# Turning attention's output with VectorE and SBUF transfers instead of TensorE, padded k and v tails, and g_norm folded into the weights

## The chip, the cores and the metric

One Trainium2 chip; the kernel runs on one of its cores. Times are device microseconds (us) of that core. Each kernel was run several times, and each experiment beside runs of the kernel before on the same chip. All profiled runs were in the fast state, and a ratio uses fast runs alone (one run each of `warm2` and `one_step` was slow; their medians include it). A ratio is the mean time of one kernel's fast runs over that of the kernel before's fast runs of the same rounds, with a 95% interval, so it is not quite the ratio of the medians that are quoted beside it. Edits are shown shortened to the lines that matter, with comments of mine behind `#`.

## The reference, cut to what matters

Eight batches, eight heads, 576 rows (S), head size 64. The convolution weights, `w_val` and `w_out` arrive as float64.

```python
kv  = einsum('bhsd,bhse->bhde', k, v)            # linear attention
raw = einsum('bhsd,bhde->bhse', q, kv)
x   = raw / sqrt(mean(raw*raw, -1) + 1e-6) * g_norm    # per head
x   = x.transpose(0, 2, 1, 3).reshape(B, S, 512)
gate = sigmoid(causal convolution of x, 5 taps per channel)
val  = x @ w_val
out  = (gate * val) @ w_out
```

## The kernel before

Everything downstream of x needs it turned: channels on partitions, rows along the free axis (`xT`). The 576 rows of a batch are four chunks of 128 and a tail of 64. TensorE turns a chunk against an identity, ScalarE copies it out of PSUM and multiplies by `g_norm` on the way:

```python
def turn_x(b, c):                                   # TensorE
    px = ps("tp", [P, NK, P], f"xTps{b}_{c}")
    for col in range(heads(c) * D // P):
        nc.tensor.transpose(px[:, col, :], st["x", b, c][:, col * P:(col + 1) * P], ident[:])
def keep_x(b, c):                                   # ScalarE
    nc.scalar.activation(out=xTs[b % 3][:, :, first:first + m], in_=px..., func=AF.Copy, scale=gcol[:])
```

The kernel does not write its instructions in program order. Each piece of work is entered into a planner with an engine, an assumed duration, a wanted time, what it needs and which buffers it takes. The planner lays out all pieces and the kernel then issues them in that order; each engine runs its own list strictly in order. This is the part of it that matters here (`t` counts in the assumed clock):

```python
plan.add("POOL", 1.75 * part, t + 2.3, powers, b, c, ...)      # rt = ss ** -0.5
plan.add("DVE",  0.7 * part,  t + 4.2, normalise, b, c, ...)   # x = raw * rt
plan.add("PE",   0.55 * part, t + 5.5, turn_x, b, c, ...)
plan.add("ACT",  0.72 * part, t + 6.2, keep_x, b, c, ...)
# [cut] the gate of a channel block: one ScalarE copy, four VectorE taps, one ScalarE sigmoid
# [cut] val (TensorE, 3 PSUM banks), gv = val * gate (VectorE, frees the bank), out (TensorE)
first = begin - (28.0 if b == 1 else 34.0)          # attention wanted 34 us ahead of val
attention(b + 1, first, 3.0, first - 8.0, first - 7.0)
gates(b + 1, first + 20.5, 6.5)
```

So a chain runs raw, square, ss, rt, x, xT, gate, taps, gv; and the fourth `val` of a batch needs the bank that the first `gv` gives back.

## Time and profile before

| | |
|---|---|
| time, median of 3 runs | 371.3 us |
| span of the profiled run | 367.9 us (timed at 369.6 us, so one of the fastest) |
| TensorE busy | 346.4 us, 94% of it |
| granted TensorE clock | 0.983 |

The prediction below shows the lines that carry the diagnosis. From the view by stretches of time (window in us, its length, TensorE's busy time and matmul count, granted clock, DMA share, GB/s): from the first `out` to the end TensorE idles 272.40 - 267.72 = 4.7 us.

```profile
95.50:367.90 272.40, 267.72 (x1316) 1.00 0.38 104
```

The timeline: start, length, engine, line, operation; in brackets the idle time just before and what ended it.

```profile
41.93 2.21 PE L481 MATMUL val<-xT,wval 128*128 128x288 f32 x8 [1.13 <-DVE gv L490]
...
75.75 3.63 PE L481 MATMUL val<-xT,wval 128*128 128x288 f32 x8 [5.01 <-DVE gv L490]
```

Behind a wait of 1.13 us eight instructions take 2.21 us, behind one of 5.01 us they take 3.63. (In the chain, where a piece ends when the next begins, such a group is the 1.94 us of the prediction; lengths of the timeline are compared with 2.21.)

### The profile page before, as it was taken

How to read it: one execution, taken by the hardware profiler on the slowest of the kernel's cores; microseconds unless marked ns; L12 is line 12 of the kernel's file. 1: busy time of each engine (PE TensorE's matmuls, PEld its weight loads, DVE VectorE, ACT ScalarE, POOL GpSimd, SP SyncE). 2: the span in 40 equal slices, each digit the busy share in tenths (PEclk: the TensorE clock that was granted, in tenths of full speed). 3: DMA queues.
4: the chain of work that ended last, by engine and by line, in shares of the span. 5: the costliest groups of instructions: out<-in, count | busy, mean ns of one | idle time of the engine just before them, and what ended most of it. 6: DMA issues, size and time to landing. Idle time of an engine off the chain costs nothing.

```text
span 367.9 us, 5562 instructions
## 1 busy us (share of the span) xinstructions
PE 346.4 (94%) x2065; PEld 234.1 (64%) x2065; DVE 215.9 (59%) x363; ACT 142.6 (39%) x253; POOL 72.4 (20%) x78
## 2 busy tenths in 40 slices
PE   4889899679799999999999999999999999999994
PEld 3677777557455784578546884678546884674441
DVE  2077998989825996927239765937249545920000
ACT  3377657535335335311353235213253335201111
POOL 0045035101430351004400350005300350000000
PEclk9969999989999999999999999999999999999998
DMA  6999975912017941793128903692121001201322
GB/s 216 318 303 351 278 222 190 276 37 64 10 48 203 269 122 40 219 276 91 30 64 250 288 22 94 173 298 59 29 66 50 2 0 50 65 2 29 86 71 72
DMA packets 43194, 49.02 MB, mean 133 GB/s; under 512 B 14475, under 2 KB 34975, under 8 KB 43167
## 3 DMA queue, kind: packets, MB, share of 16 engines
q1 hardware_dynamic: 43006, 48.67, 47.4%
q8 instruction: 16, 0.26, 0.3%
q14 instruction: 12, 0.09, 0.1%
q10 hardware_dynamic: 160, 0.00, 0.0%
HBM read 39.21 MB, written 9.44 MB: 132 GB/s over the span
## 4 chain that ended last, share of the span: by engine, by line
PE 85%; DMA 5%; SPq 3%; DVE 3%; ACT 2%; issue 1%; ACTq 0%
PE val L481 34%; PE out L500 33%; PE raw L398 8%; PE kv L329 6%; DMA v<-in_v_dram 4%; PE xTps L444 4%; SPq L193 1%; DVE gate L469 1%; SPq L203 1%; PE qTps L359 1%; DVE gv L490 1%; DMA out_dram<-ot 0%; SPq L246 0%; ACT L476 0%; ACT gate L476 0%
## 5 line engine op out<-in xcount | busy, mean ns | idle before, releaser
L481 PE MATMUL val<-xT,wval 128*128 128x288 f32 x512 | 135.5, 413 | 6.7 <-DVE gv L490 6.1
L500 PE MATMUL out<-wout,gv 128*128 128x512 f32 x288 | 126.4, 592 | 0.0
L469 DVE SCALAR_TENSOR_TENSOR gate<-xT,cwT,gate 128x576 f32<-128x576 f32 x128 | 102.9, 816 | 30.8 <-ACT gate L463 28.0
L481 PEld LDWEIGHTS val<-xT,wval 128*128 128x128 f32 x512 | 94.7, 192 | 33.5 <-DVE gv L490 7.2
L426 POOL TENSOR_TENSOR rt<-ss,mhalf 128x8 f32<-128x8 f32 (+1 forms) x40 | 63.9, 1603 | 225.1 <-DVE ss L420 225.1
L500 PEld LDWEIGHTS out<-wout,gv 128*128 128x128 f32 x288 | 53.5, 190 | 60.9 <-issue 60.7
L508 ACT COPY ot<-out 128x512 f32<-128x512 f32 x36 | 21.0, 583 | 82.0 <-PE out L500 49.9
L490 DVE TENSOR_TENSOR gv<-val,gate 128x288 f32<-128x288 f32 x64 | 28.8, 454 | 32.8 <-PE val L481 32.2
L398 PE MATMUL raw<-kvbd,qT 128*128 128x128 f32 (+1 forms) x320 | 41.2, 290 | 0.9 <-ACT kvbd L339 0.9
L451 ACT ACTIVATE xT<-xTps,gcol 128x512 f32<-128x512 f32 (+1 forms) x40 | 25.8, 644 | 39.2 <-PE xTps L444 39.2
L398 PEld LDWEIGHTS raw<-kvbd,qT 128*128 128x128 f32 (+1 forms) x320 | 37.1, 190 | 6.1 <-issue 3.6
L412 ACT ACTIVATE sq<-raw 128x512 f32<-128x512 f32 (+1 forms) x40 | 22.2, 555 | 37.4 <-PE raw L398 37.1
L476 ACT ACTIVATE gate<-gate 128x576 f32<-128x576 f32 x32 | 21.8, 682 | 35.3 <-DVE gate L469 35.2
L433 DVE TENSOR_TENSOR x<-raw,rt 128x512 f32<-128x512 f32 (+1 forms) x40 | 25.2, 629 | 17.2 <-POOL rt L426 17.0
L420 DVE TENSOR_REDUCE ss<-sq 128x8 f32<-128x520 f32 (+1 forms) x40 | 25.4, 634 | 16.0 <-ACT sq L412 15.7
L444 PE MATMUL xTps<-ident,x 128*128 128x128 f32 x144 | 22.3, 274 | 2.2 <-DVE x L433 2.2
L444 PEld LDWEIGHTS xTps<-ident,x 128*128 128x128 f32 x144 | 17.7, 141 | 10.2 <-issue 6.3
L329 PE MATMUL kv<-v,k 128*64 128x64 f32 x512 | 22.1, 230 | 1.7 <-DMA v<-in_v_dram 1.7
L329 PEld LDWEIGHTS kv<-v,k 128*64 128x64 f32 x512 | 17.9, 139 | 8.5 <-issue 7.3
L463 ACT ACTIVATE gate<-xT,cwT 128x576 f32<-128x576 f32 x32 | 22.2, 764 | 0.3
L347 DVE STREAM_TRANSPOSE qT<-q 128x576 f32<-128x576 f32 x24 | 18.0, 764 | 1.7 <-DMA q<-in_q_dram 1.7
L359 PE MATMUL qTps<-ident,q 128*64 128x128 f32 (+1 forms) x160 | 11.5, 306 | 4.7 <-DMA q<-in_q_dram 4.4
(50 smaller groups left out, 98.0 us busy)
## 6 DMA issues: line engine op xcount, KB each, us to landing
q<-in_q_dram SPq DMA_DIRECT2D x96, 140.0 KB, 4.3
out_dram<-ot SPq DMA_DIRECT2D x144, 64.0 KB, 1.7
k<-in_k_dram SPq DMA_DIRECT2D x16, 512.0 KB, 4.4
v<-in_v_dram SPq DMA_DIRECT2D x16, 512.0 KB, 6.4
q<-in_q_dram SPq DMA_DIRECT2D x4, 512.0 KB, 5.8
w_wval<-in_moe_w_val_dram SPq DMA_DIRECT2D x4, 512.0 KB, 7.9
w_wout<-in_moe_w_out_dram SPq DMA_DIRECT2D x4, 512.0 KB, 6.5
kl<-in_k_dram SPq DMA_DIRECT2D x16, 64.0 KB, 5.3
```

The source lines that it names most:

```text
L329: nc.tensor.matmul(kvp[r * D:(r + 1) * D, hp, :], st["k", b, half][:, h, j, :] if j < NJ else kl[r * T:(r + 1) * T, hp, :], st["v", b, hal ...
L398: nc.tensor.matmul(raw[row * m:(row + 1) * m, col * P:(col + 1) * P], st["qT", b][:, hp, c * P:c * P + m], kv_bd[b % 2][:, hp, :], start=T ...
L412: nc.scalar.activation(out=sq[:, 0:n, 0:D], in_=st["raw", b, c][:, 0:n * D].rearrange("p (h e) -> p h e", h=n), func=AF.Square,)
L420: nc.vector.reduce_sum(out=ss[:, 0:n], in_=st["sq", b, c][:, 0:n], axis=AX.X)
L426: nc.gpsimd.tensor_tensor(out=rt[:, 0:n], in0=st["ss", b, c][:, 0:n], in1=mhalf[:, 0:n], op=ALU.pow)
L433: nc.vector.tensor_tensor(out=x[:, 0:n * D].rearrange("p (h e) -> p h e", h=n), in0=st["raw", b, c][:, 0:n * D].rearrange("p (h e) -> p h ...
L444: nc.tensor.transpose(px[:, col, :], st["x", b, c][:, col * P:(col + 1) * P], ident[:])
L451: nc.scalar.activation(out=xTs[b % 3][:, :, first:first + m], in_=px.rearrange("p (k t) -> p k t", k=NK), func=AF.Copy, scale=gcol[:],)
L469: nc.vector.scalar_tensor_tensor(out=gate[:], in0=xTs[b % 3][:, jt, tap * TB:tap * TB + S], scalar=cwT[:, tap, jt:jt + 1], in1=gate[:], op ...
L481: nc.tensor.matmul(val[:], wval[:, kc, jt * P:(jt + 1) * P], xTs[b % 3][:, kc, HALO + n * SV:HALO + (n + 1) * SV], start=(kc == 0), stop=( ...
L490: nc.vector.tensor_tensor(out=gv[:, jt, first:first + SV], in0=st["val", b, jt, n][:], in1=st["gate", b, jt][:, n * SV:(n + 1) * SV], op=A ...
L500: nc.tensor.matmul(po[:], gv[:, jt, c * P:(c + 1) * P], wout[:, jt, :], start=(jt == 0), stop=(jt == NK - 1),)
```

## The change

Its intent: TensorE is the bound, so take work from it.

- For batches 2 to 7 the four full chunks of x are no longer turned by TensorE. VectorE turns each 32x32 block in place (`y`), and 16 SBUF-to-SBUF transfers per batch, issued by GpSimd, put the blocks where `xT` wants them. For that the rows must lie in another order, so q's turn is cut from one instruction into five.
- The 64-row tails of k and v are padded with zeros to 128 partitions, so that their matmuls have the shape of the others.
- `g_norm` goes into the convolution weights and `w_val`, as the multiplication sat in ScalarE's copy, which goes.
- To make room, buffers of x go from 3 to 2, of gate from 5 to 4, of the float64 weights from 4 to 3.

```diff
-tails = [[const.tile([P, HP, D], FP32, ...
+tails = [[const.tile([P, H, D], FP32, ...          # rows T:P cleared once
-            for r in range(2):
-                nc.sync.dma_start(out=tails[b % 2][n][r * T:(r + 1) * T], in_=...[r, SF:S])
+            nc.sync.dma_start(out=tails[b % 2][n][0:T], in_=src[b, :, SF:S, :].rearrange("h s d -> s h d"))
...
-        nc.vector.transpose(out=new_qT(b)[:, hp, :], in_=st["q", b, hp][:, :, 0:TB])
+        for c in range(NJ):
+            nc.vector.transpose(out=qT[:, c * P:(c + 1) * P], in_=q[:, c:NJ * HB:NJ, 0:TB])
+        nc.vector.transpose(out=qT[:, SF:S], in_=q[:, NJ * HB:NB, 0:TB])
...
+    def turn_blocks(b, c):
+        nc.vector.transpose(out=st["y", b][:, :, c, :], in_=st["x", b, c][:].rearrange("p (k i) -> p k i", i=TB))
+    def move_blocks(b, a):
+        for i in range(HB):                          # HB = 4
+            nc.gpsimd.dma_start(out=xTs[b % 3][i * TB:(i + 1) * TB, :, first:first + P],
+                                in_=y[a * TB:(a + 1) * TB, i])
...
+            for n, a in enumerate(range(HB - 1, -1, -1)):
+                plan.add("POOL", 2.4, t + 2.4 * n, move_blocks, b, a,
+                    needs=[("y", b, c) for c in range(NJ)]
+                    + [("xT", b, NJ) if n == 0 else ("moved", b, n - 1)],
+                    gives=[("xT", b, a), ("moved", b, n)], ..., load=0.26 / RATE)
```

Note the last entry: the 16 transfers are four pieces, and each piece is planned only once the one before has landed. The planner may put other GpSimd work between them.

## The prediction

> **What bounds the kernel now.** I read the engine table, the chain of work that ended last, the costliest groups, the chain in order of time and the timeline of one steady batch. The page first:
>
> ```profile
> PE 346.4 (94%) x2065; PEld 234.1 (64%) x2065; DVE 215.9 (59%) x363; ACT 142.6 (39%) x253; POOL 72.4 (20%) x78
> ...
> PE 85%; DMA 5%; SPq 3%; DVE 3%; ACT 2%; issue 1%; ACTq 0%
> ...
> L481 PE MATMUL val<-xT,wval 128*128 128x288 f32 x512 | 135.5, 413 | 6.7 <-DVE gv L490 6.1
> L500 PE MATMUL out<-wout,gv 128*128 128x512 f32 x288 | 126.4, 592 | 0.0
> L426 POOL TENSOR_TENSOR rt<-ss,mhalf 128x8 f32<-128x8 f32 (+1 forms) x40 | 63.9, 1603 | 225.1 <-DVE ss L420 225.1
> L347 DVE STREAM_TRANSPOSE qT<-q 128x576 f32<-128x576 f32 x24 | 18.0, 764 | 1.7 <-DMA q<-in_q_dram 1.7
> ```
>
> TensorE is busy 94% and makes 85% of the chain; `val` waits only 6.1 us for VectorE, all of it before 95 us. POOL is 20% busy. So any TensorE work removed from batches 2 to 7 pays in full, but only while nothing new makes TensorE wait. What a group really costs is in the chain in order of time (start, length):
>
> ```profile
> 219.77 0.44 PE xTps L444 x4
> 220.21 3.44 PE out L500 x8
> 223.65 0.44 PE xTps L444 x4
> 224.08 10.30 PE out L500 x24
> 234.39 1.94 PE val L481 x8
> 236.33 1.75 PE kv L329 x40
> 238.08 2.14 PE val L481 x8
> ```
>
> Turning one chunk of x is 0.44 us, an `out` chunk 3.44, a `val` group 1.94, and 2.14 behind `kv`. The timeline shows where slack is:
>
> ```profile
> 195.44 0.33 PE L329 MATMUL kv<-vl,kl 64*64 64x64 f32 x4
> 195.70 0.69 PE L329 MATMUL kv<-v,k 128*64 128x64 f32 x16
> 196.31 0.20 PEld L329 LDWEIGHTS kv<-vl,kl 64*64 64x64 f32 x4
> ...
> 219.34 1.64 POOL L426 TENSOR_TENSOR rt<-ss,mhalf 128x8 f32<-128x8 f32 x1 [1.63 <-DVE ss L420]
> ...
> 221.01 0.69 DVE L433 TENSOR_TENSOR x<-raw,rt 128x512 f32<-128x512 f32 x1 [0.74 <-POOL rt L426]
> ...
> 224.89 2.77 ACT L463 ACTIVATE gate<-xT,cwT 128x576 f32<-128x576 f32 x4
> 225.70 10.70 DVE L469 SCALAR_TENSOR_TENSOR gate<-xT,cwT,gate 128x576 f32<-128x576 f32 x13 [4.00 <-ACT gate L463]
> ```
>
> The last x of a batch is done at 221.7, its gate starts 3.2 us later, its first tap runs at 225.7 and its first `val` at 234.4. So the gate leads `val` by 8.7 us. Three PSUM banks hold `val` and `out`; the fourth `val` needs the first `gv`, which needs a finished gate. A path from x to xT longer by more than some 9 us shows up on TensorE unless the order of work changes too.
>
> **What the Trainium skill says.** "DMA: Bandwidth & Descriptors", section "Anatomy of one DMA — SWDGE (gpsimd) path": a transfer issued from GpSimd has about 2.0 us fixed cost; its section on latency gives about 1 us to the first byte, the cores' own emission. No transfer of the kernel before is issued from there, so this trace cannot confirm it. "TensorEngine Tiling (Array Packing)", section "Key Properties": changing the tiling mode drains TensorE. The trace agrees: `val` takes 2.14 instead of 1.94 us behind the 64*64 tails. "VectorE: DVE Perf Modes", section "The TRN2 errata": a fixed cost per instruction. The trace agrees: 576 columns at the page's 0.96 GHz are 600 ns, the transpose takes 764, so 164 ns are fixed. "SBUF — State Buffer", section "Who interferes with whom": a VectorE instruction with two SBUF inputs contends with GpSimd reads, and descriptor generation is put on the write side. Here `rt` has a median of 1.64 us and a longest of 2.16, so I add nothing.
>
> **The change, part by part.**
> Tails: 16 full `kv` matmuls take 0.62 us (195.70 to 196.31), the 4 tail passes 0.26 (195.44 to 195.70). At the full ones' 39 ns the four would take 0.16: 0.10 us per head pair, 3.2 us for all 32, plus about 0.1 per switch to `val` (my estimate). The first three batches lie among other waits, so I count 3 us. Half the tail transfers fall away, which SyncE feels but TensorE hardly does.
> x turns: 6 batches x 4 chunks x 0.44 = 10.6 us of TensorE go, and 24 ACT copies of 0.69 (16.5 us, ACT is not the bound).
> VectorE gains 24 block turns of 164 + 512/0.96 = 0.70 us = 16.7 us, and each q turn is cut into five: 4 x 0.30 + 0.23 = 1.43 instead of 0.76, 24 times, 16 us. Together 249 us, under 70% of the span.
> POOL gains 96 transfers of 64 KB, 16 per batch. Their issue time m is unknown; the diff's planner enters 2.4 us for four, m = 0.6, the skill's first byte suggests 1.0. I carry both.
> g_norm in the weights costs nothing: the same instructions with another scalar.
> So the gain on TensorE is 10.6 + 3 = 13.6 us.
>
> **The new path, and why I expect it to cost more.** From a finished x: block turn 0.7, then 16m of issue with the halo (1.2) among them, 2.0 landing: 13.5 us (m = 0.6) to 19.9 (m = 1) against 3.2. The kernel's list of work reacts: `raw` of the next batch moves ahead of `val`. But POOL's list then mixes the moves of one batch with `rt` of the next, and VectorE's list puts the next batch's last sums behind this batch's gates. I followed the changed program's lists with the row durations above (sq 0.6, ss 0.69, rt 1.64, x 0.68, tap 0.823, gv 0.46).
> Batch 4, counting from its `raw` 3 of batch 5 on TensorE (t = 0). The moves of the last quarter of batch 4 stand on POOL behind `rt` 3 of batch 5: square, sum and rt end at 3.3; four moves end at 3.3 + 4m; then `rt` 2 and `rt` 1 of batch 5 (3.3) and x 1 (0.7), which stands on VectorE ahead of the gate: 7.3 + 4m. Nine taps (7.4) stand ahead of the first `gv` (0.5): 15.2 + 4m, i.e. 17.6 to 19.2. TensorE has meanwhile three `val` (5.8), xTps and `raw` (2.0), kv (3.1) and two `raw` held for x 2 and x 1; it is through at 12.4. It waits 5.4 to 6.9 us, then 1.5 and 0.7 for the second and third `gv` as VectorE alternates taps and `gv` at 3.4 to 4.3 us per gate against 2 us of `val`: 7.6 to 9.1.
> The same steps for the others, m = 0.6 to m = 1: batch 2 (its last quarter stands behind `rt` 1 of batch 3, `raw` of batch 4 behind that) 11.9 to 13.5; batch 3 nothing, its `val` comes late; batch 5 (16 moves behind the x 0 that waited for the gates of batch 4) 2.1 to 8.3; batch 6 (as batch 4) 11.8 to 13.7; batch 7 (as batch 5, with only four `out` to hide behind) 5.8 to 12.1. Sum of new waits: 39.2 to 56.7.
> Net: 39.2 - 13.6 = +25.6 us, to 56.7 - 13.6 = +43.1. On 371.3: 397 to 414. I take 405.
>
> **Rivals.**
> First: the moves hide and TensorE's saving is all there is, 371.3 - 13.6 = about 358. For it: 17 us of `out` stand between the last `raw` and the first `val` in the kernel before, and POOL has 80% free. Against it: 13.5 to 20 us of path plus the interleaved `rt`, x and gate exceed that, and the slack measured is 8.7 us.
> Second: the waits are there but shorter (moves under 0.4 us, small transposes overlapping), so that gain and loss cancel: 365 to 380. For it: TensorE's order did change to cover the path. Against it: in batches 2, 4 and 6 the wait is hung on `rt` of the next batch rather than on m; with m = 0 I still get some 25 us.
> Third: issue on POOL is far dearer, 1.5 us or held up by the taps. One batch's loop (taps and `gv` 17, sum to x 3, turn, 16m, halo, landing and gate start 5) is then 26 + 24 = 50 us against 38.5 of TensorE work: about 430.
> Fourth: VectorE becomes the bound. 249 us say no in total; in the stretch of gates and `gv` it paces `val`, which is in the sum above.
>
> **Range and chances.** The two ends of m give 397 and 414; errors of my hand-followed lists, some 10 us either way, give 384 to 424. Slower by over 2% (above 378.7) needs waits above 21 us: 0.86. Within 2%: 0.08. Faster: under 6 us of waits, 0.06.
>
> **What would show it.** TensorE busy near 333 us and lower as a share (about 83%); `val` idle before it, released by `gv`, grown from 6 to 40 us or more, most of it before the fourth to sixth `val` of batches 2, 4 and 6; xTps down to 48 matmuls; tails at the full matmuls' pace; POOL's transfers at 0.6 to 1.0 us start to start; VectorE's block turns near 0.70 and cut q turns near 0.30. I am wrong if the four moves behind `rt` take well under 2 us, if `gv` is not what releases `val`, or if gates start before the next batch's x is done.

## The result, and the profile after

| | before | after |
|---|---|---|
| median | 371.3 us | 410.8 us (406.6 to 411.8) |
| ratio of fast runs | | 1.1052 [1.097, 1.1134] |
| span of the profiled run | 367.9 us | 408.5 us |
| TensorE busy | 346.4 us | 346.2 us |
| granted clock | 0.983 | 0.924 |

Slower by 39.5 us, within the range. From the page of the changed kernel: the engine table, the granted clock by slices (tenths), the chain that ended last, and three groups.

```profile
PE 346.2 (85%) x1969; PEld 231.5 (57%) x1969; DVE 235.9 (58%) x484; ACT 124.8 (31%) x229; POOL 127.5 (31%) x178
...
PEclk9979999799999955999999789999999689968999
...
PE 58%; DVE 15%; DMA 11%; SPq 6%; POOL 4%; issue 2%; ACT 2%; POOLq 0%; DVEq 0%; ACTq 0%
...
L505 PE MATMUL val<-xT,wval 128*128 128x288 f32 x512 | 145.6, 442 | 35.3 <-DVE gv L514 34.6
...
L476 POOL DMA_DIRECT2D xT<-y x96 | 53.0, 559 | 11.3 <-issue 9.5
...
L355 DVE STREAM_TRANSPOSE qT<-q 128x128 f32<-128x128 f32 x96 | 20.9, 276 | 9.2 <-DMA q<-in_q_dram 9.2
```

TensorE has 96 matmuls less and is not a microsecond less busy. `val` now idles 34.6 us behind `gv` (6.1 before), and its own busy time went from 135.5 to 145.6 us. The stretches say where; each but the first is about one batch's attention and gates, the last is the final run of `out`:

```profile
0.00:98.90 98.90, 76.27 (x752) 0.93 0.77 210
98.90:168.00 69.10, 59.15 (x288) 0.85 0.72 188
168.00:212.00 44.00, 44.00 (x224) 1.00 0.59 154
212.00:248.00 36.00, 26.93 (x231) 0.91 0.60 161
248.00:306.00 58.00, 55.56 (x231) 1.00 0.28 68
306.00:338.00 32.00, 23.20 (x96) 0.84 0.11 25
338.00:376.00 38.00, 33.65 (x97) 0.87 0.23 56
376.00:408.50 32.50, 27.42 (x64) 0.99 0.25 65
```

Length less busy time is idle: 10.0, 0, 9.1, 2.4, 8.8 and 4.4 us for batches 2 to 7. Where the idle time is long, the granted clock, the column behind the matmul count, is low. The 40.6 us more of span split so: the idle time after the first `out` is 39.7 instead of 4.7 us (+35.0); TensorE's busy time after it 269.9 instead of 267.7 (+2.2); the first `out` begins at 98.9 instead of 95.5 (+3.4).

Batch 4 shows how a wait arises. First the chain in order of time, around its first `gv`:

```profile
214.78 1.63 POOL rt L435
216.42 1.64 POOL xT L476 x3
218.06 7.13 DMA xT<-y
...
225.29 0.78 ACT gate L487
...
233.50 0.38 DVE gv L514
...
233.92 3.76 PE val L505 x8
```

The last moves of batch 4 stand behind an `rt` of batch 5, land after 7.13 us while k, v and q are being loaded, and only then can the gate start. The timeline of VectorE shows that the landing had a twin that ended at the same time:

```profile
225.04 0.69 DVE L442 TENSOR_TENSOR x<-raw,rt 128x512 f32<-128x512 f32 x1 [0.18 <-POOL rt L435]
...
226.10 7.40 DVE L493 SCALAR_TENSOR_TENSOR gate<-xT,cwT,gate 128x576 f32<-128x576 f32 x9 [0.37 <-ACT gate L487]
```

That x is of batch 5. It stands ahead of batch 4's taps in VectorE's list and ends at 225.73, when `gate`, released at 225.2, is ready at 226.07. Then nine taps, of which only four belong to the first gate, stand ahead of the first `gv`, and `val` starts 7.39 us late, at half its pace: 3.76 us.

### The profile page after: what moved, and what is told of

Its sections match the earlier page's. It is cut to its first block, busy times and chain, and to the rows that moved or that the text cites. A ratio compares the mean times of both kernels' runs of the same rounds, so it can differ in the third digit from the quotient of the medians.

```text
span 408.5 us, 5673 instructions
## 1 busy us (share of the span) xinstructions
PE 346.2 (85%) x1969; PEld 231.5 (57%) x1969; DVE 235.9 (58%) x484; ACT 124.8 (31%) x229; POOL 127.5 (31%) x178
## 4 chain that ended last, share of the span: by engine, by line
PE 58%; DVE 15%; DMA 11%; SPq 6%; POOL 4%; issue 2%; ACT 2%; POOLq 0%; DVEq 0%; ACTq 0%
PE out L524 26%; PE val L505 25%; DVE gate L493 8%; DMA v<-in_v_dram 5%; DMA xT<-y 5%; PE raw L407 5%; SPq L199 3%; POOL xT L476 2%; SPq L208 2%; DVE gv L514 2%; PE kv L334 2%; POOL rt L435 2%; DVE ss L429 1%; SPq L250 1%; DVE qT L355 1%
## 5 line engine op out<-in xcount | busy, mean ns | idle before, releaser
L505 PE MATMUL val<-xT,wval 128*128 128x288 f32 x512 | 145.6, 442 | 35.3 <-DVE gv L514 34.6
L505 PEld LDWEIGHTS val<-xT,wval 128*128 128x128 f32 x512 | 103.2, 207 | 71.2 <-DVE gv L514 40.0
L435 POOL TENSOR_TENSOR rt<-ss,mhalf 128x8 f32<-128x8 f32 (+1 forms) x40 | 63.0, 1578 | 201.5 <-DVE ss L429 201.5
L476 POOL DMA_DIRECT2D xT<-y x96 | 53.0, 559 | 11.3 <-issue 9.5
L407 PE MATMUL raw<-kvbd,qT 128*128 128x128 f32 (+1 forms) x320 | 43.3, 298 | 9.9 <-DVE x L442 5.5
L407 PEld LDWEIGHTS raw<-kvbd,qT 128*128 128x128 f32 (+1 forms) x320 | 38.6, 196 | 17.4 <-issue 7.0
L355 DVE STREAM_TRANSPOSE qT<-q 128x128 f32<-128x128 f32 x96 | 20.9, 276 | 9.2 <-DMA q<-in_q_dram 9.2
L334 PE MATMUL kv<-v,k 128*64 128x64 f32 x512 | 20.8, 227 | 3.0 <-DMA v<-in_v_dram 3.0
L468 DVE STREAM_TRANSPOSE y<-x 128x512 f32<-128x512 f32 x24 | 17.0, 709 | 0.6
L368 PEld LDWEIGHTS qTps<-ident,q 128*64 128x64 f32 (+1 forms) x160 | 10.4, 167 | 6.7 <-POOL vl L183 4.1
```

The costliest lines, as they stand in the source:

```text
L334: nc.tensor.matmul(kvp[r * D:(r + 1) * D, hp, :], st["k", b, half][:, h, j, :] if j < NJ else kl[:, 2 * hp + r, :], st["v", b, half][:, h, ...
L355: nc.vector.transpose(out=qT[:, c * P:(c + 1) * P], in_=q[:, c:NJ * HB:NJ, 0:TB])
L407: nc.tensor.matmul(raw[row * m:(row + 1) * m, col * P:(col + 1) * P], st["qT", b][:, hp, c * P:c * P + m], kv_bd[b % 2][:, hp, :], start=T ...
L435: nc.gpsimd.tensor_tensor(out=rt[:, 0:n], in0=st["ss", b, c][:, 0:n], in1=mhalf[:, 0:n], op=ALU.pow)
L476: nc.gpsimd.dma_start(out=xTs[b % 3][i * TB:(i + 1) * TB, :, first:first + P], in_=y[a * TB:(a + 1) * TB, i])
L505: nc.tensor.matmul(val[:], wval[:, kc, jt * P:(jt + 1) * P], xTs[b % 3][:, kc, HALO + n * SV:HALO + (n + 1) * SV], start=(kc == 0), stop=( ...
```

## The experiments

Theory: the way from x to a gate has become longer than the lists leave room for, and the lists put next-batch work (`rt`, x) into it. That makes waits, and long waits make TensorE slow afterwards. Rivals: the issue of the transfers on GpSimd costs this much by itself; or the tails' transfers do, or the landing.

### One part at a time

`tails`: the kernel before with the padded tails alone.

```diff
-    kl[r * T:(r + 1) * T, hp, :]
+    kl[:, 2 * hp + r, :]          # and vl; loads and clearing as in the change
```

> The kernel before with the zero-padded tails alone. My prediction's account: 3 us of TensorE saved, so 368 to 369 us, provided the start is not hurt. Rival (seen in the trace of the changed kernel, where the first out began 3.4 us later than before): the padded tails are loaded in two transfers of 128 KB that write 64 partitions each instead of four of 64 KB that write 128 between them, the start waits for loads, and the loss there is 2 to 4 us, which leaves 370 to 373 us. First val near 34.0 instead of 31.8 us under the rival, 31 to 32 under the prediction's account.

Measured: 367.7 us, ratio 0.9897 [0.987, 0.9924], 3.8 us gained (1.03% of 371). The first `val` starts at 32.4 us, so the start loses 0.6, not 2 to 4: the rival's loss does not come from the tails. The `kv` of two head pairs, 1.75 us in the prediction's chain, takes:

```profile
234.20 1.32 PE kv L330 x40
235.51 2.14 PE val L482 x8
```

That is some 0.2 us less per pair, where I had counted 0.10, and TensorE is busy 339.8 instead of 346.4 us. So 6.6 us of work go, not 3; but about half of them lie before the first `out` (75.6 instead of 78.7 us busy), which starts only 0.4 us earlier. My 3 us fit the time because two errors offset each other. And `val` behind `kv` still takes 2.14 us, so this part was not owed to the 64*64 form, as I had read it.

`tails_split`: the same, but even heads' tails in the lower 64 partitions and odd heads' in the upper, by four transfers as before.

```diff
+    out=tails[b % 2][n][r * T:(r + 1) * T, r:H:2],   # r = 0, 1; the other half cleared once
```

> The kernel before with zero-padded tails whose even heads lie in partitions 0 to 63 and odd heads in 64 to 127, each half's complement zero, loaded by the four transfers of before. If the partitions that the tail transfers write are what delays the start, the first val comes back to 31 to 32 us and the whole gains the 2 to 3 us of TensorE: 367.5 to 369.5. If the delay comes from anything else (the set-up, the order of loads), this run equals the one with the tails in the low half.

Measured: 365.7 us, ratio 0.986 [0.9825, 0.9895], below the 367.5 to 369.5 that I expected. The first `val` is back at 31.7 us. The two intervals overlap, so the 0.4% (1.4 us) between the two layouts is not certain; `early` and `early2` use this one.

`gnorm`: the kernel before with g_norm in the weights alone.

```diff
-    in0=split(mf), scalar=2.0 ** -20,
+    in0=split(mf), scalar=gcol[:] if key[0] == "wval" else 2.0 ** -20,
```

> The kernel before with g_norm multiplied into the weights alone. My prediction: costs nothing, so 370.5 to 372 us, ratio 1.00 within half a per cent. Rival: the start is what it touches (the last step of narrowing wval now waits for the convolution weights), and the first val comes later by 1 to 2 us, 372 to 373.

Measured: 371.1 us, ratio 1.000 [0.9983, 1.0016]. It costs nothing, as predicted. In its profile the first `val` is at 33.2 us, 1.4 later than before, as the rival had it; but the time shows no such loss, and the profiled run of the kernel before was a fast one.

`xturn`: the changed kernel with the tails of before (this keeps the turn and g_norm).

```diff
-            nc.sync.dma_start(out=tails[b % 2][n][0:T], ...        # and "SP", 1.3 in the plan
+            for r in range(2): nc.sync.dma_start(out=tails[b % 2][n][r * T:(r + 1) * T], ...   # "SP", 2.6
```

> The changed kernel with the tails of before: the turn of x and g_norm in the weights alone. Main theory (the longer path from x to xT and the order of work around it make TensorE wait in batches 2, 4, 6, 7, and the long waits also lower the granted clock): 406 to 414 us, all of the loss, with val's idle time released by gv at 30 to 40 us and the granted clock near 0.92. Rival (the tails carry a good part of the loss by their slower loads): under 400 us.

Measured: 419.2 us, ratio 1.1301 [1.1254, 1.1348]. All of the loss is the turn's. But it is worse than the changed kernel by 2.5% (9 us), and the tails are worth only 3.8 of that, which neither side expected.

`xturn_list`: the same instructions, with only the assumed time of the tail load set back to 1.3, which gives every engine the changed kernel's list.

```diff
-                    "SP", 2.6, want, load_tails, b, ...
+                    "SP", 1.3, want, load_tails, b, ...
```

> The turn of x with the tails of before, but with the tail load entered in the plan at 1.3 us as in the changed kernel, so that every engine has exactly the changed kernel's order of work. The turn alone took 419.2 us, 8.4 more than the changed kernel, while the padded tails alone gain 3.3 to 5. If the rest is the order that the plan makes of the other entry (main theory: order is what costs), this run takes 410.8 + 3.3 to 5, that is 413 to 416. If the tails' instructions themselves interact with the turn, it stays at 418 to 421.

Measured: 412.5 us, ratio 1.1125 [1.1103, 1.1146]. The tails are worth 1.1125 - 1.1052 = 0.7%, some 3 us (the two intervals overlap, so this is uncertain), and one assumed number that changes no instruction, only the order, is worth 1.1301 - 1.1125 = 1.8%, 6.5 us. The order is a cost of its own.

### The clock after a wait

`warm`: the changed kernel, with matmuls without a use in the four long waits.

```diff
+        if jt == 0 and n == 0 and b in WARM:        # WARM = {2: 12, 4: 16, 6: 15, 7: 8}
+            fill = ps("tp", [P, NK, P], f"fill{b}")
+            for _ in range(WARM[b]):
+                nc.tensor.matmul(fill, ident[:], wout[:, 0, :], start=True, stop=True)
         val = ps("mm", [P, SV], f"val{b}_{jt}_{n}")
```

> The changed kernel with 12, 16, 15 and 8 matmuls without a use (128x512 each, some 0.43 us) put into TensorE's long waits of batches 2, 4, 6 and 7, just ahead of the val that waits for a gv. Clock theory (the wait of over 6 us costs a second time, because the val behind it runs at a lower granted clock, 4.2 us for eight matmuls instead of 1.94): val busy falls from 145.6 to 136 to 138 us, the mean granted clock rises from 0.924 to 0.97 or more, and the time falls by 5 to 10 us to 401 to 406. Rival (after the wait, gv paces val whatever TensorE's clock): val's busy time falls but its waits grow by as much, and the time stays within 2 us of 410.

Measured: 416.5 us, ratio 1.1234. `val` fell to 132.7 us busy and the clock rose to 0.978, but the filling was sized wrong: each matmul runs as two passes of 0.43 us, so it was twice as long as I meant and overran the waits. The run says nothing on the total. Repeated with half of them:

`warm2`: as `warm`, with `WARM = {2: 6, 4: 8, 6: 7, 7: 4}`.

> The changed kernel with the idle matmuls again, now 6, 8, 7 and 4 of them: the first try showed that each 128x512 one runs as two passes of 0.43 us, so that they overran the waits by some 19 us while val still fell to 132.7 us busy. Clock theory: with 5.2, 6.9, 6.0 and 3.4 us they fit the waits of 6.1, 7.4, 7.1 and 3.8, val stays near 133 to 136 us busy, and the time falls by 6 to 10 us below the changed kernel's 410.8, to 401 to 405. Rival (gv paces val behind a wait whatever the clock): val's waits grow by what its busy time loses, and the time is 409 to 413.

Measured: 400.3 us, ratio 1.0771 [1.0722, 1.082]: 2.8% of 371, 10.4 us less than the changed kernel, by adding work. Two groups of its view by line, and the first `val` of batch 6 that waits for a `gv`, in the changed kernel and then here:

```profile
L513 PE MATMUL val<-xT,wval 128*128 128x288 f32 x512 | 133.0, 413 | 13.6 <-DVE gv L522 12.8 <-DVE wval L296 0.8
...
L508 PE MATMUL fill<-wout,ident 128*128 128x512 f32 x50 | 23.2, 616 | 0.0
```

```profile
324.84 4.21 PE L505 MATMUL val<-xT,wval 128*128 128x288 f32 x8 [7.12 <-DVE gv L514]
```

```profile
318.09 2.21 PE L513 MATMUL val<-xT,wval 128*128 128x288 f32 x8 [1.11 <-DVE gv L522]
```

TensorE's busy time is 354.8 us; less the 23.2 of filling it is 331.6, against 346.2 in the changed kernel. So some 14.6 us of busy time in the changed kernel were the same work at a lower clock. The Trainium skill, "TensorE: Matmul & The Clock Gate", Part 1, describes this: after about 3.4 us without work TensorE's clock is halved, and it takes about 3.4 us of work to get it back. The traces agree: waits of 3.80 to 7.39 us were followed by eight instructions in 3.75 to 4.21 us instead of 2.21.

### Issue and landing against order

`quarter`: the changed kernel's list, but of each four transfers only one is issued (xT is cleared at the start). Its output is wrong, which doesn't matter for the time.

```diff
-        for i in range(HB):
+        for i in (a,):
             nc.gpsimd.dma_start(
```

> The changed kernel with the same order of work, but of every four transfers from y to xT only one is issued (a wrong result on purpose; xT is cleared at the start). Main theory (the order sets the waits: the moves and the gate stand behind the next batch's rt and x, so that even free moves leave some 25 us of waits): the issue of a step falls from 2.2 to 0.55 us, the time by 8 to 15 us, to 396 to 403. Rival one (issue on GpSimd and the moves' own traffic are the cost): waits nearly vanish, under 385. Rival two (the slow landing of over 6 us beside the loads is the cost): as rival one, since a quarter of the traffic is left, but the landing medians must then fall well below 2.7 us.

Measured: 404.4 us, ratio 1.0906 [1.0853, 1.0958], so 5.4 us (1.5%) for three quarters of all issue and traffic. The clearing of xT may hide about 1 us more (the first `val` starts at 35.1 instead of 33.9). I had given 8 to 15: in this order, issue and landing matter less than I thought. The landing median is still 2.1 us (2.7 in the changed kernel). `val` still waits 30.8 us for `gv` (34.6). Batch 4 again, as the chain in order of time:

```profile
220.08 1.64 POOL rt L436
221.72 0.03 issue
221.75 0.06 DVE x L443
...
222.35 0.82 DVE gate L494
...
230.17 3.70 PE val L506 x8
```

There is no transfer in it any more. The taps now stand directly behind `rt` and x of the next batch, and `val` waits 6.93 us instead of 7.39. Moves with a quarter of the issue leave nearly the whole wait.

`act_moves`: the changed kernel with the transfers issued by ScalarE, its list made anew.

```diff
-            nc.gpsimd.dma_start(                      # "POOL", 2.4 in the plan
+            nc.scalar.dma_start(                      # "ACT", 0.4
```

> The changed kernel with the 96 moves issued by ScalarE instead of GpSimd (the list is made anew for it, with 0.4 us entered for four). Main theory: the gates still stand behind the next batch's rt and x in the list, so moving the issue elsewhere gains little: 400 to 415 us with gv still the main releaser of val. Rival (GpSimd's issue time and the mixing with rt on that one engine is the cost): 375 to 392.

Measured: 427.2 us, ratio 1.1505 [1.1475, 1.1535]. Both sides missed. Lines of its waits by engine (total us, times, longest):

```profile
PE val L505 <- DVE gv L514: 32.6, 11, 7.6
PE raw L407 <- DVE qT L356: 15.3, 4, 6.4
```

The wait for `gv` is hardly less without any transfer on GpSimd, so GpSimd's queue alone does not make it; but the list is another one, so this is no clean test. The new 15.3 us come from q that is turned late in this list, and `xTps` waits a further 11.5 us for x; why the planner put q's loads so late I did not follow up.

`one_step`: the 16 transfers of a batch entered as one piece, with nothing between them.

```diff
-            for n, a in enumerate(range(HB - 1, -1, -1)):
-                plan.add("POOL", 2.4, t + 2.4 * n, move_blocks, b, a, needs=... ("moved", b, n - 1) ...)
+            plan.add("POOL", 2.2 * HB, t, move_all, b,
+                needs=[("y", b, c) for c in range(NJ)] + [("xT", b, NJ)],
+                gives=[("xT", b, a) for a in range(HB)], frees=[("y", b)], load=0.26 / RATE)
```

> The changed kernel with all 16 moves of a batch as one step of the list, so that nothing of the next batch (rt) can stand between them, and they do not wait for one another's landing in the plan. Main theory (order): the gates start earlier, the waits for gv shrink by 10 to 16 us, and the time is 393 to 402. Rival (issue time and landing are the cost, whatever stands between): rt is held up by 8.8 us instead, TensorE waits for x in place of gv, and the time is 407 to 415.

Measured: 386.0 us, ratio 1.037 [1.0328, 1.0412]: 25 us less than the changed kernel, more than the 10 to 16 that I had given to order, with the same 96 transfers. The clock is 0.965, `val` 139.6 us busy, and its waits are:

```profile
PE val L509 <- DVE gv L518: 14.7, 6, 5.8
PE val L509 <- DMA xT<-y: 6.4, 4, 3.1
```

The longest wait for `gv` in batches 2, 4 and 6, which was 6.06, 7.39 and 7.12 us, is gone, 2.33 and 0.48; in batch 7 it is 4.54 instead of 3.80. The planner made the whole list anew, so the 25 us are those of the new order, not of the closed gaps alone. Nor are all gaps closed: in batches 2 to 5 GpSimd, after 8 to 11 transfers, waits for landings before it issues the next (8.3 us in nine waits; why is not shown). The transfers land later now, as the median of 4.5 us (2.7 in the changed kernel) shows, and the time still falls by 25 us:

```profile
xT<-y POOLq DMA_DIRECT2D x96, 64.0 KB, 4.5
```

### Making room

`early`: as `one_step`, with the attention of each batch wanted 12 us earlier, the gates later in proportion, the q turn entered at 1.1 us, and the tails split.

```diff
-            first = begin - (28.0 if b == 1 else 34.0)
+            first = begin - (28.0 if b == 1 else 46.0)
-            gates(b + 1, first + 20.5, 6.5)
+            gates(b + 1, first + 28.0, 6.5)
```

> All moves as one step, and beyond that the attention of each batch is wanted 12 us earlier (46 instead of 34 us ahead of its val) and its gates accordingly, the tails laid in both partition halves. Main theory (only the distance between x and val is too short; TensorE's saving is there): waits for gv under 10 us in batches 2 to 7, the granted clock back above 0.97, 350 to 368 us, faster than the kernel before. Rival (VectorE with its block turns, q turns, taps and gv or the transfers cannot keep up at this pace): over 378 us with waits moved to x or gv.

Measured: 366.2 us, ratio 0.9898 [0.9844, 0.9951], `val` waiting 5.6 us for `gv` in all, TensorE busy 335.0 us. The changed kernel's instructions in another order (with the split tails) are 1.0% faster than the kernel before, though not faster than the split tails alone.

`early2`: the list tuned further; the planner may also enter a piece up to 20 instead of 12 us before its wanted time.

```diff
-            first = begin - (28.0 if b == 1 else 46.0)
-            loads_kv(b + 1, first - 28.0)             # loads_q: 27.0
+            first = begin - (28.0 if b == 1 else 54.0)
+            loads_kv(b + 1, first - 34.0)             # loads_q: 33.0
-            gates(b + 1, first + 28.0, 6.5)
+            gates(b + 1, first + 29.0, 7.0)
-                    "DVE", 0.46, t + 2.0, gated, b, jt, n,
+                    "DVE", 0.46, t - 6.0, gated, b, jt, n,   # and small shifts of rt, q and kv
```

> The early attention with its list tuned further: attention wanted 54 us ahead of val, loads 6 us earlier, the gates and gv wanted so that VectorE takes a ready gv before the taps of later gates. If what is left above TensorE's work (335 us busy, and some 22 us of start) in the early run is still order, 356 to 362 us, faster than the kernel before and than the padded tails alone (365.7). If it is the landing of the moves or VectorE, no better than the early run's 366.

Measured: 365.9 us (361.3 to 366.3), ratio 0.9834 [0.9794, 0.9874]: it beats the kernel before by 1.7%, and by median it misses the 356 to 362 that I had given it. So the rival of that expectation, the landing of the moves or VectorE, is not refuted for what is left; after 96 us the chain that ended last runs for 11.8% through landings of the moves. It is level with the padded tails alone (365.7, ratio 0.986), whose interval overlaps. One row of the view by stretches each, from 95 us to the end, `tails_split` first, then `early2`, whose profiled run (363.0 us) was 3 us faster than its median:

```profile
95.00:363.90 268.90, 264.31 (x1317) 1.00 0.38 105
```

```profile
95.00:361.20 266.20, 256.19 (x1200) 0.99 0.47 123
```

With the turn TensorE works 256.2 instead of 264.3 us, 8.1 less, but idles 10.0 instead of 4.6. Even in the best list that I found, most of what the turn takes from TensorE comes back as waits.

## Why the prediction was right or wrong

The predicted 405 was near 410.8, and the reason, the long way from x to the gate and the order of work on it, is shown by `one_step` and `early`. That the number came so close is partly luck: its terms were not all right, and two errors of some 13 to 16 us offset each other.

- **The saving of TensorE (13.6 us): right as work, wrong as time.** The tails gave 3.8 us alone (of 6.6 us of work), g_norm cost nothing, xTps fell to 48 matmuls. But I expected 333 us busy, and it stayed at 346.2. The failing step is that a wait costs only its own length. At full clock the work is 331.6 us (`warm2` less its filling); 14.6 us were added by the low clock after the waits. The kernel before showed it once, at 75.75 us. `early` (335.0) and `early2` (332.9), with few long waits, do come near 333.
- **The new waits (39.2 to 56.7 us): right in place, too long.** Predicted waits and measured idle time of the stretch, in us: batch 2 11.9 to 13.5 and 10.0; batch 3 0 and 0; batch 4 7.6 to 9.1 and 9.1; batch 5 2.1 to 8.3 and 2.4; batch 6 11.8 to 13.7 and 8.8; batch 7 5.8 to 12.1 and 4.4. The sum is 34.6. The upper end rested on an issue time of 1 us; it measured 0.55.
- **Batch 4, step by step:** the order rt, moves, rt, x, nine taps, `gv` is the one in the trace. I counted a landing of 2.0 us; it took 7.13 beside the loads of k, v and q. There x of the next batch ended as late, so the error hardly showed. It ended some 3 us later than I counted, since `rt` did not follow the moves at once: GpSimd stood idle for 3.11 us until a sum of the next batch was ready. So `val` waited 7.39 us, not 5.4 to 6.9, and only 0.55 before its second `gv`; that the sum of 9.1 fits is partly luck.
- **"With m = 0 I still get some 25 us":** `quarter`, with a quarter of the issue, still waits 30.8 us for `gv`, 23.9 without the two waits of the first batches (1.13 and 5.81). The claim held; issue time mattered less than my two ends said.
- **VectorE:** block turns took 0.709 us (0.70 predicted). The cut q turn took 0.88 + 0.20 = 1.08 us, not 1.43, since four follow each other 0.22 us apart. VectorE is busy 235.9 us, not 249.
- **The start:** I counted no loss there; the first `out` is 3.4 us late by the two profiles. Part of that is chance: `warm` and `warm2`, which run the changed kernel's list up to there, have it at 96.9 and 98.3 us, and `gnorm`, which costs nothing, at 97.1 (95.5 in the kernel before). It is not the tails (95.1 in `tails`). The runs with the turn have 96.9 to 99.3, but `early2` has 95.6; what it costs here, and why, stays open.
- **Rivals:** the first (358) failed for lack of room, and even `early2` does not reach it. The second and third are refuted by 410.8 and the 0.55 us. The fourth, VectorE as the bound, falls as a bound of the whole (58% busy, and `early` has the same work in 366 us); but from the first tap of batch 4 VectorE works almost without a gap, and there it does pace `val`, as the prediction said.
- **Small slips in the working:** in batch 4, 17.6 - 12.4 is 5.2, not 5.4; 397 less 10 is 387, not 384; and the "17 us of `out`" hold only 13.7 us of `out`, the rest is `val` and xTps. None changes the forecast.

So the net came out as +35.0 for idle time, +2.2 for busy time, +3.4 for the start, where I had some 48 for waits and -13.6 for work.

## What to carry to other kernels

Work taken from the bound engine is gained only if what replaces it fits into the slack ahead of its consumer: compare the new path's length with that slack first, and change the order of work together with the operation. Read what stands in front of each piece in its engine's in-order list, because here a quarter of the transfers left nearly the whole wait, while all of them, entered as one piece in a new order, saved 25 us. And price a wait of several microseconds on TensorE at more than its length: here the eight matmuls after it took 3.6 to 4.2 us instead of 2.21.

## What the Trainium skill lacked or had wrong

- "TensorE: Matmul & The Clock Gate", Part 1, gives an idle window of about 3.4 us before the clock falls. Shorter waits did it here too: in `one_step` a wait of 2.33 us was followed by a `val` group of 3.88 us instead of 2.21, at a granted clock of 0.50 from 229 to 231 us. This wait stood directly behind `kv`; whether that matters is not shown. The page does say that short idle times between groups can make the clock swing, but gives no length for them.
- "DMA: Bandwidth & Descriptors", section "Anatomy of one DMA — SWDGE (gpsimd) path", puts the fixed cost at about 2.0 us. The shortest landing of 64 KB from SBUF to SBUF was near that (1.9 us), but the median was 2.7 us in the changed kernel, 4.5 with all sixteen entered together in `one_step`, and 7.13 for the last move of batch 4 beside the loads of k, v and q. The page lacks the time from one issue to the next: it was 0.55 us here. My 1 us was its time to the first byte, which is another thing.
- "VectorE: DVE Perf Modes", section "The TRN2 errata", adds a fixed cost to each instruction and does not say how much of it short instructions in a row hide. (Elsewhere the page says that an instruction which is not held starts before the one in front has ended, without a figure.) Four turns of 276 ns each took 0.88 us together.
